# Sinkhorn-sorted attention and a token mixer on one Trainium2 core: masks ahead of a copy, wider weights for one turn, fewer idle products, a split last row and a new instruction order

## The chip, the cores and the metric

One core of a Trainium2 chip. The metric is the device time of one execution in microseconds (us). The engines are TensorE (PE, with its weight loads as PEld), VectorE (DVE), ScalarE (ACT), GpSimd (POOL) and SyncE (SP, which here only issues transfers). A core has 16 DMA engines; transfers are issued from the queues of SP, ACT and POOL. PSUM has eight banks of 512 float32 per partition. TensorE alone fills them, VectorE and ScalarE empty them.

## The reference

The input is q, k and v (4 batches, 8 heads, 768 positions, 64 wide, float32), sort_net (4, 8, 8, 8) and three matrices. The first half sorts blocks of 96 positions with a soft permutation P and attends inside each block; the second mixes tokens with weights made from the attention's output:

```python
P = sort_net
for _ in range(5):
    P = np.exp(P - np.max(P, axis=-1, keepdims=True))
    P = P / (np.sum(P, axis=-1, keepdims=True) + 1e-09)
    P = P / (np.sum(P, axis=-2, keepdims=True) + 1e-09)
k_sorted = np.einsum('bhij,bhjcd->bhicd', P, k_b)      # v_sorted likewise
attn = softmax(scale * q_b @ k_sorted^T)               # per block of 96
x = attn @ v_sorted                                    # (4, 768, 512)
W_tok = scale * (x @ w_q) @ (x @ w_k)^T
out = np.maximum(W_tok @ x, 0) @ w_out
```

## The kernel before, in words

The whole program is one list, ORDER (lines 20 to 54), read word by word by the loop at lines 661 to 671. A capital letter is a group of products on TensorE, and its number behind the colon is the PSUM bank; the small letter of the same name empties that bank, on ScalarE (A), VectorE (D) or POOL (G); a word that begins with l is a load issued by POOL. The first digit is the batch, the rest says which part. So K20:6 is the sorted k of batch 2, head pair 0, into banks 6 and 7, and k20:A its copy by ScalarE. Each engine takes its words in the order of the list, and waits there until what a word needs is ready; a word that waits holds up all later words of its engine. Bank numbers and engines are written out by hand for each word.

The groups that the change or the prediction's steps touch:

- **a and c** (lines 171 and 183): the softmax chain that makes P. a is an exponential on ScalarE, c the sums, reciprocals and products on VectorE; they alternate five times. A (line 179) makes a small mask m_p; Z (line 257) multiplies zeros (idle products; the last digits of the name count them, so Z04 is four).
- **I, z, Q, q** (lines 266, 342, 262 and 274): q of batch 0 comes by I, two transfers from SP's queue; z1n casts it; Q turns one head pair by an identity product, and q copies it to QT. For batches 1 to 3 the copy p (line 271) puts the two heads of a pair side by side first; it waits for POOL's load lq.
- **B, u, n** (lines 235, 242, 245): B00 spreads P over 128 partitions in one bank. u00 copies that bank to PTR in SBUF on ScalarE. n makes the masks M that sort k and v: those of batch 0 (n00 to n03, two heads each) read the bank itself, on VectorE; those of batches 1 to 3 read PTR, on POOL.
- **K/k, Y/y, F/f, V/v, R** (lines 289 to 331): sorted k; sorted v of batch 0, which is turned once more by F; sorted v of the other batches (V), moved to VT by six transfers R on SP's queue.
- **S/e, P/r/x** (lines 352 to 395): scores in seven groups and their exponentials; the products with v in five groups, the reciprocal of the sums and the product that makes X.
- **T/t or D, J/j, d, W/w, G/g, H/h** (lines 397 to 462): X is turned on TensorE (T) or by a transposing transfer (D); J makes q' and k' (qkT, 64 rows each); d moves k' to the other half of the partitions (qD); W turns k' back in eight blocks of 96 columns, by a product with an identity; G and H make the mixed and rectified tokens, mixT.
- **O/o/s** (lines 464 to 488): the last product in six rows per batch, its copy out of PSUM and its store. For batch 3 each row has its own store. A number from 10 up means half of a row's columns (osplit), so 325 is the second half of row 5 and 315 the first half.

POOL's loads go into three buffers each of q, k and v (NIN, line 112), each half of a batch (four heads) by itself: lk0a is the first half of k of batch 0. At the end POOL checks the reciprocals (guard, line 495); with this input the slow path behind it isn't taken.

Of the kernel before, what the change touches and what calls it, by code (L numbers as in the profile page):

```python
# [17 lines left out]
VHEAD = set()  # L18

ORDER = """  # L20
i00:G i02:D I00:S A00:0 lv0b I01:S Z04:1 lk0a c00:D a01:A i03:G c01:D lv0a a02:A:0 lk0b c02:D z11:A
lv1b lv1a a03:A Q01:0 c03:D lk1a z10:A a04:A c04:D Z22:1 z12:A Q00:2 q01:D:0 a05:A z13:A Z32:3 c05:D
q00:A:2 Q03:0 Z52:1 q03:D:0 B00:2 Q02:3 u00:A:2 n01:D:2 Z12:0 n00:D:2 n11:G K01:4 n03:D:2 K00:0
q02:D:3 k01:A:4 Y03:6 n10:G k00:D:0 y03:A:6 S02:4 n02:D:2 e02:A:4 Y00:0 lq1b K02:2 Y02:6 y00:A:0
k02:D:2 Y01:4 lk1b y02:A:6 S00:0 y01:D:4 lp K03:2 e00:A:0 S01:6 k03:D:2 F00:4 lq1a e01:A:6 F01:5
f00:D:4 S06:2 S05:0 e06:A:2 f01:D:5 P00:6 e05:A:0 S03:2 r00:D:6 x00:D:6 V12:4 e03:A:2 P01:0 r01:D:0
x01:D:0 v12:A:4 S04:6 F03:2 F02:3 e04:A:6 R15:S V11:4 f02:D:3 V10:0 v11:A:4 f03:D:2 P02:6 p12:G
Z42:3 v10:A:0 r02:D:6 x02:D:6 R12:S p13:G Z62:4 P04:2 R14:S K11:4 n20:G T00:0 r04:D:2 x04:D:2
k11:A:4 R13:S Q12:1 P03:6 R11:S t00:A:0 q12:D:1 lk2a K13:2 r03:D:6 x03:D:6 R10:S Q13:1 k13:A:2 lv2b
K12:4 U00:0 k12:A:4 lv2a K10:2 z01:D:0 T03:6 q13:D:1 k10:A:2 T02:7 t03:D:6 U01:4 p11:G T01:5 t02:D:7  # L30
z02:A:4 S16:2 S14:0 t01:D:5 lo e16:A:2 S15:6 Q11:4 e15:A:6 p10:G J01:5 q11:D:4 J00:2 e14:A:0 n21:G
S13:6 j00:D:2 j01:A:5 Q10:0 e13:A:6 W01:1 lq2a W00:1 P14:2 P13:4 w00:A:1 d01:G r14:D:2 x14:D:2
q10:A:0 K20:6 lq2b G00:1 r13:D:4 x13:D:4 k20:A:6 lq3a S11:2 G01:1 e11:A:2 d00:G K21:6 g00:D:1 S10:4
lk2b k21:D:6 H01:0 e10:A:4 h01:D:0 V20:2 V21:4 v20:A:2 V22:6 v21:D:4 P10:0 v22:A:6 R21:S T13:2
r10:D:0 x10:D:0 R20:S H02:4 S12:6 O02:3 R25:S e12:A:6 h02:D:4 R23:S H00:0 o02:A:3 P12:6 R22:S
h00:A:0 O03:3 p21:G r12:D:6 x12:D:6 R24:S t13:A:2 P11:4 lk3a O04:0 r11:D:4 x11:D:4 p20:G O00:2
o04:A:0 lv3a p23:A T10:0 o00:D:2 lv3b Q21:1 p22:A Q20:4 q21:D:1 T11:2 n31:G q20:A:4 T12:5 t11:D:2
O05:1 t12:A:5 o03:D:3 lq3b t10:D:0 S22:6 S20:4 e22:A:6 S21:2 lk3b o05:D:1 J11:0 p30:G e21:A:2 Q23:1
j11:D:0 J10:6 p31:G q23:D:1 e20:A:4 Q22:7 j10:D:6 W11:1 n30:G Q30:0 q22:A:7 K22:4 q30:D:0 K23:2
k22:A:4 Q31:0 s01:G k23:D:2 W10:1 P21:6 d10:G w10:A:1 d11:D S23:4 q31:D:0 S24:2 e23:A:4 O01:1  # L40
r21:D:6 x21:D:6 e24:A:2 S25:4 G10:0 o01:D:1 e25:A:4 K31:6 K30:2 k31:D:6 G11:0 k30:A:2 P22:4 g10:D:0
S26:2 r22:D:4 x22:D:4 V30:0 e26:A:2 P23:6 v30:A:0 H10:2 r23:D:6 x23:D:6 V31:4 h10:A:2 R30:S p33:G
S31:0 R31:S v31:D:4 e31:A:0 p32:G V32:6 H12:2 v32:A:6 S32:0 h12:D:2 R33:S Q33:4 Q32:5 e32:A:0 R32:S
K32:6 q33:D:4 R34:S P24:2 k32:A:6 K33:0 r24:D:2 x24:D:2 R35:S k33:A:0 P20:6 q32:D:5 D21:S H11:2
S35:0 r20:D:6 x20:D:6 h11:A:2 O14:5 e35:A:0 S33:2 o14:D:5 D20:S S36:6 O13:4 e33:A:2 P31:0 s00:S
e36:A:6 S34:2 r31:D:0 x31:D:0 P34:6 e34:A:2 O10:5 r34:D:6 x34:D:6 P32:2 o10:A:5 S30:0 r32:D:2
x32:D:2 P33:6 e30:A:0 J20:5 J21:0 r33:D:6 x33:D:6 j20:A:5 P30:2 d20:G j21:A:0 W20:5 r30:D:2 x30:D:2
d21:G W21:5 D31:S O12:6 w20:A:5 G21:5 o13:D:4 D30:S G20:5 o12:D:6 O11:4 g20:D:5 s11:S H20:6 s02:S
H22:2 h20:A:6 H21:0 h22:D:2 O15:5 o11:A:4 O21:6 o15:D:5 h21:A:0 s10:G O20:7 J30:0 J31:1 j30:D:0
O25:5 d30:G j31:D:1 d31:S W30:4 o20:D:7 W31:4 O22:1 w30:A:4 w31:A:4 o25:D:5 o21:A:6 G31:0 s12:A  # L50
G30:0 s20:A O23:6 o22:A:1 g30:A:0 H30:0 o23:D:6 H31:4 h30:A:0 H32:2 h31:D:4 O24:7 s21:S h32:A:2
O31:6 o24:A:7 O32:2 o31:D:6 s22:S O34:3 s31:A o32:D:2 O35:6 s32:A o34:A:3 O30:7 o35:D:6 s34:S O33:3
s35:A o30:D:7 s30:S o33:A:3 s33:S
"""


# [1 line left out]
def kernel(  # L58
# [23 lines left out]
    DH = moe_w_q.shape[1]  # L82
# [40 lines left out]
    qkT = tiles("qkT", 2, [P, S])  # L123
# [6 lines left out]
    q32 = [x.rearrange("p t s -> p (t s)").bitcast(FP32).rearrange("p (h r d) -> p h r d", r=R6, d=D) for x in XT]  # L130
# [10 lines left out]
    idb = sb.tile([P, P], BF16, name="idb")  # L141
# [11 lines left out]
    def mm(o, w, x, start=True, stop=True, t=False):  # L153
        nc.tensor.matmul(o, w, x, is_transpose=t, start=start, stop=stop, skip_group_check=True)  # L154
# [267 lines left out]

    def u_W(b, n, bank):
        for i in range(4 * n, 4 * n + 4):
            mm(PS[0:BLK, bank, i * DH:(i + 1) * DH], qkT[b % 2][:, i * BLK:(i + 1) * BLK], idb[:, DH:P])

    def u_w(b, n, e, bank):
        i0, i1 = (4 * n, 4 * n + 4) if b == B - 1 else (0, NB)
# [232 lines left out]
    for item in ORDER.split():  # L661
# [5 lines left out]
        b, n = int(name[1]), int(name[2:])  # L667
# [41 lines left out]
```

## Time and profile before

| | us |
|---|---|
| median of 3 timed runs | 99.87 |
| lowest and highest | 98.56, 100.75 |
| the profiled execution's own time | 98.28 |
| its span in the profile | 96.3 |
| busy in it: PE, PEld, DVE, ACT, POOL | 83.7, 57.7, 72.4, 68.8, 43.1 |

The profile lists the instructions of one execution, grouped by line, engine and shape, or in order of time. A row of the timeline has start, duration, engine, line, operation, what it writes and reads, and in brackets how long its engine had stood idle before it and what ended that. Line 154 is the helper through which all products go, lines 158, 160 and 162 those of the copies, so these rows are told apart by the names of their tiles. "fil" is the tile of zeros that the idle products use. Neighbouring rows of one group are merged, with a count behind the x.

### The profile page before, as it was taken

What the parts mean: (1) busy time and instruction counts of PE and PEld (TensorE: products, weight loads), DVE (VectorE), ACT (ScalarE), POOL (GpSimd) and SP (SyncE); (2) the same over time, 40 slices, a digit from 0 to 9 for tenths busy, and PEclk for the clock granted to TensorE, in tenths of its full rate; (3) what the DMA queues carried; (4) which work ended last, traced back from release to release, by engine and by line L of the source; (5) the groups of instructions that cost most, each with busy time, mean ns of one, the idle gap of its engine ahead of it and who ended that gap; (6) DMA issues with size and microseconds to landing.
All of it is one profiled execution on the core that took longest, in us unless ns stands there. A gap on an engine that the chain in (4) does not pass through costs nothing.

```text
span 96.3 us, 3183 instructions
## 1 busy us (share of the span) xinstructions
PE 83.7 (87%) x1322; PEld 57.7 (60%) x1332; DVE 72.4 (75%) x141; ACT 68.8 (72%) x96; POOL 43.1 (45%) x70
## 2 busy tenths in 40 slices
PE   4429488999999999899999999899989999999930
PEld 2024177888788687855868687675666645644400
DVE  2667987988799469999777999998698773645520
ACT  5267739998789899886989898999766090466220
POOL 6993069800999994049999004200004021950000
PEclk9999999999999999999999999999999999999999
DMA  1899999999999999999999999659961998385992
GB/s 10 262 356 228 203 202 203 203 202 208 194 276 229 208 205 206 202 202 232 251 231 204 202 205 274 188 140 218 180 244 32 225 353 361 119 354 221 395 367 113
DMA packets 24656, 21.44 MB, mean 223 GB/s; under 512 B 7297, under 2 KB 22721, under 8 KB 24641
## 3 DMA queue, kind: packets, MB, share of 16 engines
q0 software_dynamic: 12720, 10.36, 65.6%
q1 hardware_dynamic: 11200, 9.05, 32.5%
q10 hardware_dynamic: 720, 1.84, 4.8%
q8 instruction: 10, 0.16, 0.7%
q14 instruction: 6, 0.04, 0.1%
HBM read 20.19 MB, written 6.29 MB: 275 GB/s over the span
## 4 chain that ended last, share of the span: by engine, by line
PE 58%; DVE 14%; ACT 14%; DMA 5%; issue 4%; SPq 0%; DVEq 0%; ACTq 0%
PE ps L154 58%; ACT E L363 5%; DMA XT<-in_q_dram 5%; DVE X L392 5%; ACT KT L158 3%; ACT Vs L158 3%; DVE QT L162 2%; DVE Vs L162 1%; DVE Rall L387 1%; DVE XT L162 1%; ACT mixT L460 1%; ACT Qn L158 1%; DVE tmp L193 1%; DVE Pm L190 1%; DVE tmp L189 1%
## 5 line engine op out<-in xcount | busy, mean ns | idle before, releaser
L363 ACT ACTIVATE E<-ps 96x960 bf16<-96x960 f32 (+1 forms) x28 | 24.3, 905 | 2.3 <-PE ps L154 1.6
L154 PE MATMUL ps<-wo,mixT 128*128 128x512 bf16 x88 | 22.8, 380 | 0.4
L392 DVE TENSOR_TENSOR X<-ps,Rall 96x896 bf16<-96x896 f32 (+1 forms) x20 | 20.1, 1007 | 0.7
L160 POOL COPY Qn<-Qn 128x768 bf16<-128x768 bf16 x10 | 8.1, 829 | 17.1 <-DMA Qn<-in_q_dram 17.0
L162 DVE COPY ot<-ps 128x512 f32<-128x512 f32 (+1 forms) x16 | 10.8, 687 | 4.8 <-PE ps L154 4.1
L154 PEld LDWEIGHTS <-mixT 128*128 128x128 bf16 x96 | 8.3, 98 | 9.1 <-issue 0.8
L154 PE MATMUL ps<-idb,Qn 128*128 128x128 bf16 x96 | 8.4, 231 | 4.4 <-ACT Qn L158 3.1
L158 ACT CAST KT<-ps 128x768 bf16<-128x768 f32 x13 | 10.1, 806 | 2.3 <-PE ps L154 1.8
L154 PE MATMUL ps<-VT,E 96*128 96x65 bf16 x256 | 11.1, 193 | 0.2
L154 PEld LDWEIGHTS <-E 96*128 96x128 bf16 x256 | 9.8, 97 | 2.1 <-ACT E L363 0.4
L154 PEld LDWEIGHTS <-KT 64*128 64x128 bf16 (+1 forms) x288 | 8.4, 97 | 4.1 <-issue 2.2
L154 PEld LDWEIGHTS <-Qn 128*128 128x128 bf16 x96 | 6.2, 103 | 7.5 <-ACT Qn L158 6.8
L253 POOL TENSOR_TENSOR M<-PTR,m_p 128x512 bf16<-128x512 bf16 x6 | 7.9, 1316 | 5.0 <-ACT PTR L158 4.9
L154 PE MATMUL ps<-QT,KT 64*128 64x96 bf16 x256 | 9.3, 204 | 0.7 <-ACT KT L158 0.2
L460 ACT ACTIVATE mixT<-ps 128x1024 bf16<-128x1024 f32 x7 | 7.1, 1027 | 3.5 <-PE ps L154 3.5
L160 POOL COPY qD<-qkT 64x384 bf16<-64x384 bf16 x6 | 3.0, 504 | 14.5 <-ACT qkT L158 12.2
L158 ACT COPY ot<-ps 128x512 f32<-128x512 f32 x9 | 5.3, 587 | 5.1 <-PE ps L154 4.7
L154 PE MATMUL ps<-M,Kn 128*64 128x128 bf16 x192 | 7.8, 221 | 0.3 <-DVE M L253 0.3
L158 ACT CAST Vs<-ps 128x1024 bf16<-128x1024 f32 x7 | 7.0, 1016 | 0.5 <-PE ps L154 0.3
L162 DVE CAST KT<-ps 128x768 bf16<-128x768 f32 x7 | 6.5, 952 | 1.0 <-PE ps L154 0.9
L387 DVE RECIPROCAL Rall<-ps 96x14 f32<-96x14 f32 (+1 forms) x20 | 4.6, 229 | 3.5 <-PE ps L154 1.8
L162 DVE COPY QT<-ps 128x768 bf16<-128x768 bf16 x12 | 6.6, 546 | 0.7 <-PE ps L154 0.7
(84 smaller groups left out, 140.8 us busy)
## 6 DMA issues: line engine op xcount, KB each, us to landing
Vn<-in_v_dram POOLq DMA_DIRECT2D x8, 384.0 KB, 9.6
Kn<-in_k_dram POOLq DMA_DIRECT2D x8, 384.0 KB, 10.3
out_dram<-ot SPq DMA_DIRECT2D x5, 512.0 KB, 4.6
VT<-Vs SPq DMA_DIRECT2D x18, 132.0 KB, 5.3
Qn<-in_q_dram POOLq DMA_DIRECT2D x6, 384.0 KB, 10.8
XT<-in_q_dram SPq DMA_DIRECT2D x2, 768.0 KB, 5.8
out_dram<-ot POOLq DMA_DIRECT2D x2, 512.0 KB, 7.5
out_dram<-ot ACTq DMA_DIRECT2D x2, 512.0 KB, 2.8
```

The lines of the kernel that those rows point to most:

```text
L154: nc.tensor.matmul(o, w, x, is_transpose=t, start=start, stop=stop, skip_group_check=True)
L158: nc.scalar.copy(o, i)
L160: nc.gpsimd.tensor_copy(o, i)
L162: nc.vector.tensor_copy(o, i)
L189: nc.vector.reciprocal(tmp, tmp)
L190: nc.vector.tensor_mul(Pv, Pv, rows(tmp))
L193: nc.vector.reduce_sum(tmp, (Pm if n == 1 else Pv).rearrange("p i j -> p j i"), axis=AX.X)
L253: ENG[e].tensor_tensor(out=M[b % 2][:, h0:h0 + hn], in0=src.unsqueeze(2).to_broadcast([P, hn, SP, NB]), in1=m_p.unsqueeze(1).unsqueeze(3). ...
L363: nc.scalar.activation(E[b % 2][:, n, 0:2 * w * BLK].rearrange("p (t a c) -> p a t c", a=2, c=BLK), PS[0:BLK, bank:bank + 2, 0:w * BLK].re ...
L387: nc.vector.reciprocal(Rall[:, b, n, :, 0:w], avps(bank, w)[:, :, :, D])
L392: nc.vector.tensor_mul(xo.rearrange("p (a t d) -> p a t d", a=2, d=D), avps(bank, w)[:, :, :, 0:D], Rall[:, b, n, :, 0:w].unsqueeze(3).to_ ...
L460: nc.scalar.activation(o, i, ACT.Relu)
```

## The change

- ORDER is written anew: all positions, most banks, and for 67 words the engine. Seven groups of idle products (16 products) become four (10): Z42, Z52 and Z62 are gone, the other four are placed differently. The masks n00 to n03 of batch 0 come ahead of u00. POOL's first memsets (i03) come ahead of all loads, and the loads have another order; batch 0's q comes in the order I01, I00.
- Row 5 of batch 3 (O35, o35, s35) is cut into two halves of columns (325 and 315), which come last of all; both half copies are on VectorE and both half stores on ScalarE's queue.
- u_W reads 128 columns of k' as weights instead of 96, except for each fourth block; the products write 128 rows instead of 96, of which the copy w reads 96 as before.

```diff
--- before.py
+++ after.py
@@ -18,39 +18,39 @@
 VHEAD = set()
 
 ORDER = """
-i00:G i02:D I00:S A00:0 lv0b I01:S Z04:1 lk0a c00:D a01:A i03:G c01:D lv0a a02:A:0 lk0b c02:D z11:A
-lv1b lv1a a03:A Q01:0 c03:D lk1a z10:A a04:A c04:D Z22:1 z12:A Q00:2 q01:D:0 a05:A z13:A Z32:3 c05:D
-q00:A:2 Q03:0 Z52:1 q03:D:0 B00:2 Q02:3 u00:A:2 n01:D:2 Z12:0 n00:D:2 n11:G K01:4 n03:D:2 K00:0
-q02:D:3 k01:A:4 Y03:6 n10:G k00:D:0 y03:A:6 S02:4 n02:D:2 e02:A:4 Y00:0 lq1b K02:2 Y02:6 y00:A:0
-k02:D:2 Y01:4 lk1b y02:A:6 S00:0 y01:D:4 lp K03:2 e00:A:0 S01:6 k03:D:2 F00:4 lq1a e01:A:6 F01:5
-f00:D:4 S06:2 S05:0 e06:A:2 f01:D:5 P00:6 e05:A:0 S03:2 r00:D:6 x00:D:6 V12:4 e03:A:2 P01:0 r01:D:0
-x01:D:0 v12:A:4 S04:6 F03:2 F02:3 e04:A:6 R15:S V11:4 f02:D:3 V10:0 v11:A:4 f03:D:2 P02:6 p12:G
-Z42:3 v10:A:0 r02:D:6 x02:D:6 R12:S p13:G Z62:4 P04:2 R14:S K11:4 n20:G T00:0 r04:D:2 x04:D:2
-k11:A:4 R13:S Q12:1 P03:6 R11:S t00:A:0 q12:D:1 lk2a K13:2 r03:D:6 x03:D:6 R10:S Q13:1 k13:A:2 lv2b
-K12:4 U00:0 k12:A:4 lv2a K10:2 z01:D:0 T03:6 q13:D:1 k10:A:2 T02:7 t03:D:6 U01:4 p11:G T01:5 t02:D:7
-z02:A:4 S16:2 S14:0 t01:D:5 lo e16:A:2 S15:6 Q11:4 e15:A:6 p10:G J01:5 q11:D:4 J00:2 e14:A:0 n21:G
-S13:6 j00:D:2 j01:A:5 Q10:0 e13:A:6 W01:1 lq2a W00:1 P14:2 P13:4 w00:A:1 d01:G r14:D:2 x14:D:2
-q10:A:0 K20:6 lq2b G00:1 r13:D:4 x13:D:4 k20:A:6 lq3a S11:2 G01:1 e11:A:2 d00:G K21:6 g00:D:1 S10:4
-lk2b k21:D:6 H01:0 e10:A:4 h01:D:0 V20:2 V21:4 v20:A:2 V22:6 v21:D:4 P10:0 v22:A:6 R21:S T13:2
-r10:D:0 x10:D:0 R20:S H02:4 S12:6 O02:3 R25:S e12:A:6 h02:D:4 R23:S H00:0 o02:A:3 P12:6 R22:S
-h00:A:0 O03:3 p21:G r12:D:6 x12:D:6 R24:S t13:A:2 P11:4 lk3a O04:0 r11:D:4 x11:D:4 p20:G O00:2
-o04:A:0 lv3a p23:A T10:0 o00:D:2 lv3b Q21:1 p22:A Q20:4 q21:D:1 T11:2 n31:G q20:A:4 T12:5 t11:D:2
-O05:1 t12:A:5 o03:D:3 lq3b t10:D:0 S22:6 S20:4 e22:A:6 S21:2 lk3b o05:D:1 J11:0 p30:G e21:A:2 Q23:1
-j11:D:0 J10:6 p31:G q23:D:1 e20:A:4 Q22:7 j10:D:6 W11:1 n30:G Q30:0 q22:A:7 K22:4 q30:D:0 K23:2
-k22:A:4 Q31:0 s01:G k23:D:2 W10:1 P21:6 d10:G w10:A:1 d11:D S23:4 q31:D:0 S24:2 e23:A:4 O01:1
-r21:D:6 x21:D:6 e24:A:2 S25:4 G10:0 o01:D:1 e25:A:4 K31:6 K30:2 k31:D:6 G11:0 k30:A:2 P22:4 g10:D:0
-S26:2 r22:D:4 x22:D:4 V30:0 e26:A:2 P23:6 v30:A:0 H10:2 r23:D:6 x23:D:6 V31:4 h10:A:2 R30:S p33:G
-S31:0 R31:S v31:D:4 e31:A:0 p32:G V32:6 H12:2 v32:A:6 S32:0 h12:D:2 R33:S Q33:4 Q32:5 e32:A:0 R32:S
-K32:6 q33:D:4 R34:S P24:2 k32:A:6 K33:0 r24:D:2 x24:D:2 R35:S k33:A:0 P20:6 q32:D:5 D21:S H11:2
-S35:0 r20:D:6 x20:D:6 h11:A:2 O14:5 e35:A:0 S33:2 o14:D:5 D20:S S36:6 O13:4 e33:A:2 P31:0 s00:S
-e36:A:6 S34:2 r31:D:0 x31:D:0 P34:6 e34:A:2 O10:5 r34:D:6 x34:D:6 P32:2 o10:A:5 S30:0 r32:D:2
-x32:D:2 P33:6 e30:A:0 J20:5 J21:0 r33:D:6 x33:D:6 j20:A:5 P30:2 d20:G j21:A:0 W20:5 r30:D:2 x30:D:2
-d21:G W21:5 D31:S O12:6 w20:A:5 G21:5 o13:D:4 D30:S G20:5 o12:D:6 O11:4 g20:D:5 s11:S H20:6 s02:S
-H22:2 h20:A:6 H21:0 h22:D:2 O15:5 o11:A:4 O21:6 o15:D:5 h21:A:0 s10:G O20:7 J30:0 J31:1 j30:D:0
-O25:5 d30:G j31:D:1 d31:S W30:4 o20:D:7 W31:4 O22:1 w30:A:4 w31:A:4 o25:D:5 o21:A:6 G31:0 s12:A
-G30:0 s20:A O23:6 o22:A:1 g30:A:0 H30:0 o23:D:6 H31:4 h30:A:0 H32:2 h31:D:4 O24:7 s21:S h32:A:2
-O31:6 o24:A:7 O32:2 o31:D:6 s22:S O34:3 s31:A o32:D:2 O35:6 s32:A o34:A:3 O30:7 o35:D:6 s34:S O33:3
-s35:A o30:D:7 s30:S o33:A:3 s33:S
+i00:G i02:D I01:S i03:G A00:0 I00:S Z04:1 c00:D lk0b a01:A c01:D lk0a lv0a a02:A:0 lv0b c02:D lv1b
+z13:A lv1a a03:A Q03:0 c03:D lq1b z12:A lk1b a04:A q03:A:0 Z12:1 c04:D z10:A Q02:0 a05:A z11:A Z22:1
+c05:D q02:A:0 Q00:2 q00:D:2 B00:0 Q01:1 n03:D:0 n01:D:0 q01:A:1 K03:2 n00:D:0 K01:4 k03:A:2 n02:D:0
+K00:6 k01:D:4 u00:A:0 K02:2 k00:A:6 n10:G S05:0 k02:D:2 Y01:4 e05:A:0 Y00:6 y01:D:4 S01:2 lq1a Z32:0
+e01:A:2 y00:D:6 lp S04:4 Y03:0 e04:A:4 Y02:2 n11:G S00:6 y02:D:2 y03:A:0 F00:4 F01:5 e00:A:6 f00:D:4
+lk1a S02:2 f01:D:5 V11:0 e02:A:2 n20:G S03:6 v11:D:0 S06:4 e06:A:4 P01:2 e03:A:6 F02:4 r01:D:2
+x01:D:2 R13:S p12:G V12:0 V10:6 v12:A:0 p13:G f02:D:4 P00:2 v10:A:6 Q12:5 R15:S r00:D:2 x00:D:2
+F03:4 R14:S Q13:0 q12:A:5 K13:6 R10:S f03:D:4 P02:2 k13:A:6 R12:S T00:1 q13:D:0 p11:G r02:D:2
+x02:D:2 t00:A:1 R11:S S15:6 P03:4 e15:A:6 lv2a K12:0 r03:D:4 x03:D:4 U00:2 p10:G k12:A:0 P04:6 T01:3
+lv2b S16:0 z01:D:2 S14:4 e16:A:0 r04:D:6 x04:D:6 T02:2 n21:G e14:A:4 Q11:0 U01:1 t02:D:2 Q10:6
+q11:A:0 t01:D:3 T03:7 lk2a K11:4 t03:D:7 z02:A:1 K10:2 k11:D:4 J01:7 k10:A:2 n30:G J00:1 q10:D:6
+j01:A:7 lo S10:6 j00:A:1 S11:2 e10:A:6 W01:4 W00:4 lq2a P13:0 w00:D:4 e11:A:2 S12:6 d01:G r13:D:0
+x13:D:0 G01:4 lq3a e12:A:6 G00:4 lk2b S13:2 d00:D g00:D:4 P14:0 e13:A:2 V22:6 r14:D:0 x14:D:0 V20:4
+v22:A:6 H01:2 v20:D:4 K20:0 h01:A:2 V21:6 k20:D:0 R20:S K21:4 v21:A:6 H00:2 R25:S k21:D:4 P12:0
+h00:A:2 R21:S P11:6 r12:D:0 x12:D:0 H02:4 R24:S O03:2 h02:A:4 R22:S r11:D:6 x11:D:6 P10:0 R23:S
+O02:3 p21:A p20:G r10:D:0 x10:D:0 T11:6 o02:A:3 n31:G T13:7 Q21:4 o03:A:2 Q20:5 t13:D:7 T12:2
+q21:D:4 lq2b q20:A:5 O05:7 t11:D:6 p30:A p31:G t12:D:2 S21:4 S22:0 o05:D:7 e21:A:4 S20:2 lk3b T10:6
+O04:7 lv3b e20:A:2 t10:D:6 J11:6 lv3a o04:A:7 J10:2 j11:A:6 e22:A:0 Q30:3 j10:D:2 K22:6 K23:4
+q30:A:3 k22:D:6 P21:0 k23:A:4 O00:2 r21:D:0 x21:D:0 p23:A p22:G W11:3 Q31:4 W10:3 o00:A:2 Q23:5 lk3a
+q31:D:4 P20:0 w10:A:3 q23:D:5 Q22:4 lq3b r20:D:0 x20:D:0 S26:2 S25:6 e26:A:2 s01:G G10:5 e25:A:6
+K32:2 d11:G q22:D:4 G11:5 d10:G k32:D:2 K33:0 g10:A:5 P24:6 k33:A:0 H11:4 r24:D:6 x24:D:6 H10:2
+h11:A:4 H12:0 h10:D:2 S24:6 h12:A:0 V32:4 v32:D:4 V31:2 e24:A:6 S23:0 e23:A:0 v31:D:2 V30:6 R35:S
+K31:4 R34:S v30:A:6 K30:0 k31:D:4 P22:2 R33:S k30:A:0 O11:6 r22:D:2 x22:D:2 R30:S p32:G p33:A R32:S
+P23:0 o11:A:6 S31:4 R31:S r23:D:0 x23:D:0 S30:2 e31:A:4 Q33:6 D20:S O10:7 e30:A:2 q33:D:6 Q32:0
+o10:D:7 D21:S S32:4 S36:2 q32:D:0 O01:6 e36:A:2 e32:A:4 s10:S S33:2 S34:0 e33:A:2 P30:4 O14:7
+r30:D:4 x30:D:4 e34:A:0 P31:2 o01:A:6 S35:0 r31:D:2 x31:D:2 P32:4 s00:G e35:A:0 J20:6 o14:A:7
+r32:D:4 x32:D:4 P34:0 J21:2 j20:A:6 d20:G P33:6 j21:A:2 r34:D:0 x34:D:0 D30:S W20:4 W21:4 O13:5
+w20:A:4 r33:D:6 x33:D:6 d21:A G21:4 G20:4 o13:D:5 D31:S O12:6 g20:A:4 H20:4 s02:S H21:0 h20:A:4
+H22:2 O15:7 h22:D:2 h21:A:0 O21:4 o12:D:6 o15:A:7 O23:5 s11:S s12:G J30:7 J31:6 j30:A:7 o21:A:4
+O20:0 j31:A:6 W30:4 d31:S W31:4 O22:1 w30:D:4 w31:D:4 d30:S o20:D:0 G30:4 o23:D:5 G31:4 s20:S O24:0
+o22:D:1 g30:A:4 s21:G H31:4 H32:6 h31:A:4 H30:2 O25:1 h30:D:2 o24:A:0 O33:4 o25:D:1 O30:5 o33:D:4
+s22:A h32:A:6 O32:1 s33:S o30:D:5 O31:0 s30:A o32:A:1 O34:5 o31:D:0 s32:S O325:4 s31:S o34:A:5
+O315:0 o325:D:4 s34:A o315:D:0 s325:A s315:A
 """
 
 
@@ -422,7 +422,8 @@
 
     def u_W(b, n, bank):
         for i in range(4 * n, 4 * n + 4):
-            mm(PS[0:BLK, bank, i * DH:(i + 1) * DH], qkT[b % 2][:, i * BLK:(i + 1) * BLK], idb[:, DH:P])
+            w = BLK if i % 4 == 3 else P
+            mm(PS[0:w, bank, i * DH:(i + 1) * DH], qkT[b % 2][:, i * BLK:i * BLK + w], idb[:, DH:P])
 
     def u_w(b, n, e, bank):
         i0, i1 = (4 * n, 4 * n + 4) if b == B - 1 else (0, NB)
```

## The prediction

> **What bounds the kernel now.** I read the page first (busy times, clock, the chain's shares), then busy times by stage, then the timeline at each edit. From the page:
>
> ```profile
> span 96.3 us, 3183 instructions
> PE 83.7 (87%) x1322; PEld 57.7 (60%) x1332; DVE 72.4 (75%) x141; ACT 68.8 (72%) x96; POOL 43.1 (45%) x70
> PEclk9999999999999999999999999999999999999999
> DMA  1899999999999999999999999659961998385992
> PE 58%; DVE 14%; ACT 14%; DMA 5%; issue 4%; SPq 0%; DVEq 0%; ACTq 0%
> ```
>
> TensorE is the largest share of the chain that ends last, VectorE and ScalarE are not far behind, the clock is never down, and the transfer engines are busy without a gap from slice 2 to slice 27 (about 2.4 to 65 us). Busy time by stage comes next, from the first sorted k (13.3) to the end of the last product (about 92.0); columns are start:end, length, then busy time of PE, PEld, DVE, ACT, POOL, clock, transfer share, GB/s.
>
> ```profile
> 13.30:30.60 17.30, 16.32 (x387) 14.45 (x389) 15.47 (x27) 15.42 (x20) 11.80 (x15) 1.00 1.28 215
> 59.40:73.20 13.80, 12.86 (x230) 9.23 (x231) 11.96 (x20) 11.87 (x16) 1.58 (x3) 1.00 0.80 188
> 73.20:92.00 18.80, 18.64 (x142) 9.61 (x142) 11.48 (x17) 8.26 (x14) 5.07 (x11) 1.00 0.77 275
> sum 78.70, PE 76.04 PEld 54.27 DVE 63.38 ACT 61.06 POOL 35.48; mean PE 15.21 PEld 10.85 DVE 12.68 ACT 12.21 POOL 7.10
> ```
>
> Over 78.7 us TensorE stands still for 78.70 - 76.04 = 2.7 us, almost all of it in the first row (17.30 - 16.32 = 1.0) and the second (13.80 - 12.86 = 0.9). In the first row the two engines that empty PSUM are busy for 15.47 and 15.42 of 17.30, so that stage is held by all three; in the last row TensorE alone sets the end. So a new order can win back at most 2.7 us, and there is little in it unless the two stages with gaps change.
>
> **First masks.** The timeline around the first masks:
>
> ```profile
> 11.99 0.51 DVE L162 COPY QT<-ps 128x768 bf16<-128x768 bf16 x1
> 12.12 0.36 PE L154 MATMUL ps<-PbT,Lx 32*128 32x32 bf16 x8 [0.15 <-DVE PbT L197]
> 12.51 0.37 ACT L158 CAST PTR<-ps 128x256 bf16<-128x256 f32 x1 [0.85 <-PE ps L154]
> 12.91 1.09 DVE L253 TENSOR_TENSOR M<-ps,m_p 128x256 bf16<-128x256 f32 x3 [0.42 <-ACT PTR L158]
> 13.28 0.82 PEld L154 LDWEIGHTS <-Kn 128*64 128x64 bf16 x24 [0.42 <-issue]
> ```
>
> The mask on VectorE stands idle for 0.42 us until ScalarE's copy of the same bank ends at 12.88, though it reads only the bank. In the new order the masks come first, so the copy's 0.4 us leave the path. But a q copy (0.51, the row at 11.99) now stands on VectorE between the end of the softmax chain and the masks: chain end about 12.1, plus 0.55, gives 12.65 instead of 12.91. I take -0.25 us; the bounds are -0.4 (the whole wait) and 0 (a q copy now stands on ScalarE between the fourth and the fifth exponential and could delay the chain by as much). The copy in turn now comes behind four masks, 4 x 0.36 us, and POOL's masks of batch 1 and the scores that want bank 0 come behind the copy; this takes nothing off the first sorted k, which needs only its own mask. [...]
>
> **No idle products late.** Seven groups of products into unused columns become four: six products fewer.
>
> ```profile
> 23.35 1.28 DVE L162 COPY VT<-ps 96x1024 bf16<-96x1024 bf16 x2 [0.26 <-PE ps L154]
> 24.38 0.56 PEld L154 LDWEIGHTS <-fil 128*128 128x128 bf16 x4
> 25.06 0.50 PEld L154 LDWEIGHTS <-E 96*128 96x128 bf16 x8
> ```
>
> Two of the six stand ahead of B00, in TensorE's wait for the softmax: worth 0. The other four run from 24.38 to 25.06: 0.68 us at most. The products that follow (E, eight of them) want the bank that VectorE's copy leaves at 23.35 + 1.28 = 24.63, so they could have begun 0.4 us earlier. Against that, one of the groups that stay (Z32) moves from the softmax, where it cost nothing, to a place behind the second group of scores of batch 0: two products, half of the 0.68, under a wait for a bank as far as I can follow, and up to 0.34 if that wait is gone. I take -0.3 for all of it; bounds +0.34 (VectorE, busy for 15.47 of 17.30, is the limit at 24.4 anyway and Z32 costs its full time) and -0.68.
>
> **k' turned by 128 columns.** Three of four weight loads of the turn of k' become 128 wide. By the rows of both widths:
>
> ```profile
> L154 PEld LDWEIGHTS <-qkT 128*96 128x96 bf16 x32 | 2.0, 124 | 0.3
> L154 PEld LDWEIGHTS <-mixT 128*128 128x128 bf16 x96 | 8.3, 98 | 9.1 <-issue 0.8 <-ACT mixT L460 0.5
> 73.18 0.58 PEld L154 LDWEIGHTS <-qkT 128*96 128x96 bf16 x8
> 26.07 0.37 PEld L154 LDWEIGHTS <-X 96*128 96x128 bf16 x8
> ```
>
> 24 loads x (124 - 98) ns = 0.62 us is the most, if the loads set the pace; eight 96-wide loads took 0.58, eight 128-wide ones with a similar stream 0.37. But weight loads run under the product before, and only two of the four batches (2 and 3) have the turn with little else beside it, so I take -0.1; bounds 0 and -0.6. [...]
>
> **Last row in halves.** The end now:
>
> ```profile
> 92.02 0.38 PE L154 MATMUL ps<-wo,mixT 128*128 128x512 bf16 x1
> 92.44 0.58 ACT L158 COPY ot<-ps 128x512 f32<-128x512 f32 x1 [1.63 <-PE ps L154]
> L446 DVE TENSOR_SCALAR Ab<-ps 128x256 bf16<-128x256 f32 x3 | 1.2, 417 | 0.1
> out_dram<-ot SPq DMA_DIRECT2D x3, 256.0 KB, 2.3
> qD<-qkT SPq DMA_DIRECT2D x1, 48.0 KB, 2.0
> ```
>
> The last product, copy and store become half as large; the copy moves to VectorE. No copy of 128x256 float32 to float32 is in the trace; the nearest, a 128x256 read of PSUM on VectorE, takes 0.42, so 0.58 - 0.42 = 0.16. The last store falls from 256 to 128 KB; 48 KB take 2.0 and 256 KB 2.3, so at most 0.3, and I take 0.2. Both half stores are issued by ScalarE, one behind the other; its queue has nothing else left. One product group, one copy and one store are added, the first half's copy under the second half's products. Sum -0.4; bounds 0 and -0.5.
>
> **The new order.** 67 items change their engine. The six more that ScalarE gets are 6 of 104, and VectorE's total hardly changes; the sum of emptying is not smaller than before, so the gaps can only be closed by better fitting. I found no such place by hand, and take 0 here, with -1.9 (both stages' gaps closed) as the lower bound. What I can follow is the loads. POOL's queue and the wait on batch 2's v:
>
> ```profile
> 27.11 0.82 POOL L232 DMA_DIRECT2D Kn<-in_k_dram  x1
> 29.49 0.82 POOL L160 COPY Qn<-Qn 128x768 bf16<-128x768 bf16 x1
> 35.06 0.36 PEld L154 LDWEIGHTS <-Kn 128*64 128x64 bf16 x12
> 37.86 0.51 PEld L154 LDWEIGHTS <-M 128*128 128x128 bf16 x9 [0.26 <-DMA Vn<-in_v_dram]
> L253 POOL TENSOR_TENSOR M<-PTR,m_p 128x512 bf16<-128x512 bf16 x6 | 7.9, 1316 | 5.0 <-ACT PTR L158 4.9
> DMA to landing us min/median/max: 6.5/10.3/15.0
> ```
>
> The last line is for the loads of k. Now the first half of k for batch 2 (lk2a) is issued at 27.11, ahead of the copy p11 that waits for q of batch 1 and runs at 29.49. In the new order it comes behind p11, lv2a, p10, lv2b and the mask n21: 0.82 + 0.82 + 0.82 + 0.82 + 1.32 = 4.6 us after that q has landed. q's place among the loads is one earlier, about 2 us (the transfer engines are full, so loads land one after another), so lk2a is issued at about 27.5 + 4.6 = 32.1 and lands no sooner than 32.1 + 6.5 = 38.6. Its user K20 stands later in TensorE's order too: it now begins at 35.06, and by the items now ahead of it that were behind it (S10, S11, S12, G00, G01, V20, V22, H01, less the idle products) would come near 37. V22 just ahead of K20 wants both halves of v, which are again two loads in the same queue, so TensorE arrives at 37 to 38 and may wait 0.6 to 1.6 there, against 0.26 now; all of TensorE's later work is queued behind. Some of this is absorbed, as the emptying engines go on meanwhile. I take +0.4; bounds 0 and +4.6 (a median landing, 32.1 + 10.3 = 42.4, against 37.5 and the 0.26 of now).
>
> **Sum.** -0.25 - 0.3 - 0.1 - 0.4 + 0.4 = -0.65 us. The profiled execution took 98.28 us, 96.3 of span and 2.0 around it, so the sum gives 97.6 against its own 98.28. The three timed runs have a median of 99.87 (98.56 to 100.75); the profiled one lies below all of them. The mean of the four is 99.4, the sum on that scale is 98.7, and this I give: **98.7 us**. About 2% (2.0 us) is what a measurement of this kernel can tell from no change.
>
> **Rivals.**
> The order fits better than I can see: the gaps at 13.3 to 30.6 and 59.4 to 73.2 close by 1.9 us and K20 doesn't wait. For it: in those rows no engine is full, so the waits are a matter of order; against it: ScalarE gets more, not less. Then -0.65 - 0.4 - 1.9 = -2.95: 96.4 us.
> The loads hand everything back: transfers are full from 2.4 to 65 us, the loads are the same in number and size, so what masks and idle products gain early is waited for again at the next load; only the halves and the turn remain, -0.5: 98.9 us. For it: the wait on v at 37.86; against it: it is the only such wait on TensorE after the start, and 0.26 us short.
> Slower: lk2a lands late and K20 holds TensorE up for longer than everything else gains. It decides from the point where the added wait exceeds the other gains (1.05 us), that is when lk2a lands after 37.5 + 0.26 + 1.05 = 38.8. Its price is halfway between the 0.6 and the 4.6 above, +2.6, less 1.05: +1.55, 100.9 us. For it: five POOL items moved ahead of this load, and a median of 10.3 us to landing; against it: that median was for loads issued behind a longer queue.
> That the edit does nothing: the 96-wide loads and the removed products were under other work already, and the masks' gain is eaten by the softmax chain, which has one more q copy on ScalarE inside it; the time is 99.4 less the halves' 0.4, 99.0, and its chance is counted with the second rival's.
>
> **How the numbers follow.** Forecast 0.38, better order 0.24, loads hand it back 0.20, late K20 0.18. The range reaches the better order (96.4) and the late K20 (100.9): 96.3 to 101.0, which leaves out the far halves of both, 0.12 + 0.09; the forecast's own range is 97.7 to 99.7. Faster by over 2%, a gain of 2.0 us: nearly all of the better order and a fifth of the forecast, since the base itself scatters by 1 us either way: 0.24 x 0.9 + 0.38 x 0.2 = 0.29, say 0.3. Slower by over 2% takes a wait of 3.1 us at K20, which is under half of that rival, and a little of the scatter: 0.13. The rest, 0.57, lies within.
>
> **What would show it.** Masks: the first M on VectorE begins near 12.65 with no wait on PTR, and PTR begins after the last of four. Idle products: none after 20 us. Turn: a row of qkT loads of 128 columns near 98 ns. End: a copy of 128x256 near 0.42 us last, and span end under 3.9 us after the last product. Loads: a wait of TensorE on Kn's load between 36 and 40 us of 0.6 to 1.6. The prediction is wrong if TensorE's idle time from the first sorted k to the last product is below 1.5 us or above 4.5, or if the first sorted k starts after 13.3.

## The result, and the profile after

The changed kernel takes 101.9 us (median of 4, 101.34 to 102.1) against 99.23 for the one before (98.56 to 100.75): a ratio of 1.032, 95% interval 1.026 to 1.037. It is slower; 98.7 was forecast, in a range of 96.3 to 101.0. Ratios compare, for each kernel, the executions that lie near its fastest, so a ratio can differ from the quotient of two medians; why the kernel before spreads from 98.2 to 102 is taken up in runs 7 and 9. The profiled execution of the changed kernel took 101.87, with a span of 99.9. From its page:

```profile
span 99.9 us, 3193 instructions
PE 84.8 (85%) x1321; PEld 59.9 (60%) x1330; DVE 72.0 (72%) x139; ACT 71.2 (71%) x102; POOL 41.7 (42%) x68
PEclk9999999999999999999999999999999999999985
DMA 38%; PE 24%; DVE 17%; POOL 5%; ACT 5%; issue 4%; SPq 1%; DVEq 0%; POOLq 0%; ACTq 0%
```

Less work, and yet TensorE is busy for 84.8 us instead of 83.7: something runs more slowly. The granted clock doesn't show it (1.00 in the first row below), and falls only when the products are over (0.79 in the last). The chain's share for transfers follows POOL's queue of loads and says little of the cause. Busy time by stage, the same stretches as before and the rest:

```profile
13.30:30.60 17.30, 16.80 (x357) 14.54 (x357) 14.82 (x23) 15.01 (x19) 12.86 (x15) 1.00 1.27 205
59.40:73.20 13.80, 12.05 (x223) 8.81 (x225) 11.89 (x17) 12.31 (x16) 1.37 (x2) 1.00 0.97 254
92.00:99.90 7.90, 2.14 (x14) 1.18 (x12) 1.54 (x3) 1.05 (x2) 0.00 (x0) 0.79 0.54 203
```

In the first stretch TensorE is busy for longer (16.80 after 16.32) with fewer products (357 after 387). The second has 1.75 us of standstill after 0.94; the difference is the wait for the transposed X of batch 2 at J20, first before, then changed:

```profile
PEld L154 <- DMA XT<-X: 0.5, 1, 0.5
PE ps L154 <- DMA XT<-X: 1.3, 1, 1.3
```

The third is the end: it lasts 7.9 us, in the kernel before 4.3 (96.3 - 92.0). By the last copy out of PSUM the changed kernel is 1.6 us behind (94.61 for 93.02); the other 2.0 us come after that copy.

**The start.** TensorE's timeline up to the first sorted k, first of the kernel before, then of the changed one:

```profile
6.62 0.82 PE L154 MATMUL ps<-idb,Qn 128*128 128x128 bf16 x6 [3.14 <-ACT Qn L158]
7.23 1.06 PE L154 MATMUL ps<-fil 128*128 128x512 bf16 x2
8.08 0.85 PE L154 MATMUL ps<-idb,Qn 128*128 128x128 bf16 x6
8.72 1.06 PE L154 MATMUL ps<-fil 128*128 128x512 bf16 x2
11.02 0.51 PE L154 MATMUL ps<-idb,Qn 128*128 128x128 bf16 x6 [1.24 <-DVE Pm L190]
...
13.39 0.81 PE L154 MATMUL ps<-M,Kn 128*64 128x128 bf16 x22 [0.26 <-DVE M L253]
```

```profile
6.90 0.82 PE L154 MATMUL ps<-idb,Qn 128*128 128x128 bf16 x6 [3.42 <-ACT Qn L158]
7.51 1.06 PE L154 MATMUL ps<-fil 128*128 128x512 bf16 x2
9.49 0.80 PE L154 MATMUL ps<-idb,Qn 128*128 128x128 bf16 x6 [0.92 <-ACT QT L158]
...
12.64 0.82 PE L154 MATMUL ps<-idb,Qn 128*128 128x128 bf16 x6
13.39 2.77 PE L154 MATMUL ps<-M,Kn 128*64 128x128 bf16 x48
```

The same six q products take 0.82 us until 9 us and 0.51 at 11.02 in the kernel before; in the changed one they still take 0.82 at 12.64. There 48 products of the sorted k take 2.77 us, where 22 took 0.81: pairs start every 106 ns instead of every 55. The products of the first sorted v go at the same pace until 17.8; from 18.03 on it is the full one. So TensorE works at half its rate in the changed kernel until 18 us. In the kernel before the four groups from 6.62 to 9.8 follow each other without a gap; in the changed one Q02 waits 0.92 us, from 8.57 on, for the copy of Q03, since the new order gives both bank 0.

The idle products, 512 columns wide, show two rates as well: in the kernel before their starts lie 427 ns apart at 8.72 and 216 at 11.37. The time to the rise is not one number here: 5.5 us after the last gap (12.31) in this execution, and 2.9 us in run 11. That the gaps hold the rise back is at this point the author's reading; runs 1, 4 and 9 test it.

**The end.** The first row of POOL's check in the kernel before, and then POOL's, VectorE's and ScalarE's rows of the last microseconds in the changed one:

```profile
82.14 0.76 POOL L500 CROSS_LANE_REDUCE s<-Rall 96x1 f32<-96x280 f32 x1
```

```profile
87.22 0.53 POOL L486 DMA_DIRECT2D out_dram<-ot  x1 [5.61 <-DVE ot L162]
87.81 0.76 POOL L501 CROSS_LANE_REDUCE s<-Rall 96x1 f32<-96x280 f32 x1
...
93.75 0.86 DVE L162 COPY ot<-ps 128x256 f32<-128x256 f32 x2 [0.61 <-PE ps L154]
...
93.92 1.37 ACTq L489 DMA_DIRECT2D out_dram<-ot  x3
```

POOL's check of the reciprocals started at 82.14 before. Now the stores s12 and s21 stand ahead of it on POOL; s21 waits 5.61 us for its rows and the check begins at 87.81. From the end of the last copy (93.75 + 0.86 = 94.61) to the end of the span it takes 5.3 us; before, 96.3 - 93.02 = 3.3. In the records of the trace POOL's closing instructions now end at 99.1 and the wait for the last store at 98.1; before, POOL was done at 93.4 and the wait for the last store ended at 95.3. From the check's first row to the end of POOL's closing work it is 11.3 us in both (82.14 to 93.4, 87.81 to 99.1), so that end came 5.7 us later with a check that started 5.67 us later.

### The profile page after: what moved, and what is told of

Read it like the earlier page. It is cut to its first block, busy times and chain, and to the rows that moved or that the text cites. A ratio compares the mean times of both kernels' runs of the same rounds, so it can differ in the third digit from the quotient of the medians.

```text
span 99.9 us, 3193 instructions
## 1 busy us (share of the span) xinstructions
PE 84.8 (85%) x1321; PEld 59.9 (60%) x1330; DVE 72.0 (72%) x139; ACT 71.2 (71%) x102; POOL 41.7 (42%) x68
## 3 DMA queue, kind: packets, MB, share of 16 engines
q1 hardware_dynamic: 11136, 8.57, 28.8%
## 4 chain that ended last, share of the span: by engine, by line
DMA 38%; PE 24%; DVE 17%; POOL 5%; ACT 5%; issue 4%; SPq 1%; DVEq 0%; POOLq 0%; ACTq 0%
PE ps L154 24%; DMA Qn<-in_q_dram 23%; DMA XT<-X 5%; DMA out_dram<-ot 5%; DMA XT<-in_q_dram 5%; DVE X L392 4%; POOL M L253 2%; DVE ot L162 2%; DVE VT L162 2%; POOL Qn L160 2%; DVE QT L162 1%; ACT Qn L158 1%; DVE Vs L162 1%; ACT E L363 1%; DVE Rall L387 1%
## 5 line engine op out<-in xcount | busy, mean ns | idle before, releaser
L154 PE MATMUL ps<-wo,mixT 128*128 128x512 bf16 (+1 forms) x92 | 22.5, 370 | 0.5 <-issue 0.2
L162 DVE CAST KT<-ps 128x768 bf16<-128x768 f32 x11 | 10.3, 953 | 2.5 <-PE ps L154 2.5
L461 ACT ACTIVATE mixT<-ps 128x1024 bf16<-128x1024 f32 x9 | 9.0, 1029 | 3.3 <-PE ps L154 3.3
L486 POOL DMA_DIRECT2D out_dram<-ot x4 | 2.2, 542 | 19.5 <-ACT ot L158 13.9
L162 DVE COPY ot<-ps 128x512 f32<-128x512 f32 (+2 forms) x14 | 8.9, 646 | 1.8 <-PE ps L154 1.6
L158 ACT COPY ot<-ps 128x512 f32<-128x512 f32 x12 | 6.9, 587 | 2.1 <-PE ps L154 1.9
L158 ACT CAST KT<-ps 128x768 bf16<-128x768 f32 x9 | 7.2, 800 | 0.8 <-PE ps L154 0.8
L154 PEld LDWEIGHTS <-Kn 128*64 128x64 bf16 x192 | 7.1, 125 | 1.0 <-issue 0.4
L154 PE MATMUL ps<-XT,wqk 128*128 128x384 bf16 x32 | 6.2, 326 | 1.3 <-DMA XT<-X 1.3
L158 ACT COPY QT<-ps 128x768 bf16<-128x768 bf16 x7 | 5.6, 794 | 1.8 <-PE ps L154 1.8
```

The costliest lines, as they stand in the source:

```text
L158: nc.scalar.copy(o, i)
L162: nc.vector.tensor_copy(o, i)
L461: nc.scalar.activation(o, i, ACT.Relu)
L486: ENG[e].dma_start(out=od[:, 2 * n:2 * n + 2, :], in_=oslot(b, 2 * n))
```

## The experiments

Two theories came out of this, the cold start and the late check; the rivals are given with each run. All runs were timed in five rounds beside the kernel before, runs 1 to 4, 5 to 8 and 9 to 12 on one chip each; "less than the change" is therefore a difference of two ratios, each with its own interval.

**1. The changed kernel, kept busy ahead of the first sorted k**

```diff
-... Z12:1 c04:D ... Z22:1 c05:D
+... Z14:1 c04:D ... Z24:1 c05:D
```

> The changed kernel with four idle products instead of two in each of the two groups ahead of the first sorted k (Z12 and Z22 become Z14 and Z24), so that TensorE has hardly a gap from 6.9 us on. Cold-start theory (TensorE runs at half rate until about 18 us because it is no longer kept busy before the first sorted k): pairs of K products start every 55 ns instead of 106, S01 starts at about 17.0 instead of 18.02, and the time falls by 0.7 to 1.5 us. Rival (the end is set by later waits and by the tail, so an earlier start is handed back): S01 earlier all the same, but J20 waits longer and the time falls by less than 0.4 us.

Measured: 1.012 (1.003 to 1.020), so 2.0% less than the change and more than expected. One of the seven executions took 269.31 us and one 104.41; neither is explained, and neither is in the ratio. TensorE in its profile:

```profile
12.62 0.51 PE L153 MATMUL ps<-idb,Qn 128*128 128x128 bf16 x6
13.34 1.20 PE L153 MATMUL ps<-M,Kn 128*64 128x128 bf16 x36 [0.22 <-DVE M L252]
```

36 products of k in 1.20 us, full rate, and S01 starts at 16.32 instead of 18.02. The cold start is a cause. In this profile 1.0 of the 1.7 us reaches the end of the last copy (93.63 for 94.61). Some is handed back as the rival said: TensorE's wait for the transposed X of batch 2 (J20) grows from 1.3 to 1.6 us.

```profile
PE ps L153 <- DMA XT<-X: 1.6, 1, 1.6
```

**2. The changed kernel with the check no longer behind stores**

```diff
-... s11:S s12:G ... g30:A s21:G
+... s11:S s12:S ... g30:A s21:S
```

> The changed kernel with the two stores s12 and s21 issued by SP instead of POOL, so that POOL's check of the reciprocals can start before 83 us as it did before. Theory of the late check (POOL's closing work ends last in the span): it begins about 5 us sooner and the time falls by 0.8 to 1.0 us, the end being then set by the last store. Rival (the last stores set the end in any case): less than 0.2 us.

Measured: 1.013 (1.006 to 1.020), 1.8% less than the change and twice what was expected. Its page's first line, and its last microseconds:

```profile
span 97.9 us, 3194 instructions
```

```profile
75.21 0.76 POOL L501 CROSS_LANE_REDUCE s<-Rall 96x1 f32<-96x280 f32 x1 [0.61 <-DVE Rall L387]
...
93.63 0.86 DVE L162 COPY ot<-ps 128x256 f32<-128x256 f32 x2 [0.61 <-PE ps L154]
...
93.81 1.37 ACTq L489 DMA_DIRECT2D out_dram<-ot  x3
```

The last copies and stores come at the same times as in the change (within 0.12 us); the span ends 2.0 us sooner. About 0.9 us of it is POOL's closing work, which ended 0.9 us after the last store's wait. The rest is that store itself: here its last packet is written at 96.2, in the change most are by 96.3, but some fifteen trickle in until 97.6. From the last copy to the end of the span it is 5.2 to 5.3 us in both profiles with the late check (the change, run 1) and 3.4 in all four of the new order with the early one (runs 2, 5, 6 and 12).

Why the late check slows the last store is not shown, but the transfers of the traces point to something. Two packets of 8 KB of the queue that the profile calls "instruction" follow POOL's branch behind the check. In the change (branch at 92.56) they run from 93.72 to 94.19 and from 96.84 to 97.14, among the last packets of the stores, of which none ends between 96.84 and 97.19; in run 2 (branch at 80.25) they come at 81.2 and 84.5. Run 2 also changes the queue of the two stores, and no run separates that from the check's time.

The start of this execution differs too. Its first sorted k is still cold, but the full rate is there at 16.3, and from 20 to 40 us it is 1.0 us ahead of the change; by 74 us that lead is gone. So what an earlier start is worth at the end differs from execution to execution.

**3. The kernel before with the masks first**

```diff
-... u00:A:2 n01:D:2 Z12:0 n00:D:2 n11:G K01:4 n03:D:2 K00:0
+... n01:D:2 Z12:0 n00:D:2 K01:4 n03:D:2 u00:A:2 n11:G K00:0
```

> The kernel before with only the first masks put ahead of the copy of their bank. The prediction's step: the first mask begins near 12.55 without a wait, the first sorted k 0.3 to 0.4 us earlier, the time 0.25 us less (0 to 0.4). Rival: the stage behind is held by the engines that empty PSUM, and the time doesn't move (under 0.1 us).

Measured: 1.000 (0.994 to 1.006). No gain is to be seen, but the interval doesn't exclude the 0.25 us. Run 8 shows where it goes.

**4. The kernel before without four early idle products**

```diff
-... Z22:1 z12:A ... Z32:3 c05:D
+... z12:A ... c05:D
```

> The kernel before without the idle products Z22 and Z32 (four products of 16, all before 10 us). Cold-start theory: TensorE is at half rate at 13.3 us, pairs of K products start every 106 ns, and the time grows by 0.7 to 1.8 us. Rival (these products only fill TensorE's idle time and the rate is up in any case, or the loss is made good later): less than 0.3 us.

Measured: 1.021 (1.013 to 1.028), 2.1% slower than before by this alone, a little over what was expected. TensorE in its profile:

```profile
8.05 0.82 PE L154 MATMUL ps<-idb,Qn 128*128 128x128 bf16 x6 [0.58 <-ACT Qn L158]
...
12.98 0.82 PE L154 MATMUL ps<-idb,Qn 128*128 128x128 bf16 x6
...
14.58 0.64 PE L154 MATMUL ps<-M,Kn 128*64 128x128 bf16 x8
```

The first sorted k comes at 14.58 instead of 13.39, its pairs 106 ns apart. Four products whose results nobody uses, in time that TensorE has to spare, are worth 2 us against the executions of the kernel before in which the rate is up in time.

**5. The changed kernel with both repairs**: the diffs of 1 and 2 together.

> The changed kernel with both repairs, the longer idle groups ahead of the first sorted k (Z14, Z24) and the stores s12 and s21 on SP. If the cold start and the late check are separate causes and make up the loss, the gains add: 1.032 - 0.020 - 0.018 = 0.994 of before, 98.6 us, within 0.6. Rival (both are paid out of the same 2 us at the end, or a third cause holds the end): 1.01, no better than either alone.

Measured: 1.002 (0.997 to 1.006), median 98.91. The gains of 1 and 2 add up to 3.8% and 3.0% are measured: between the two theories, nearer to the sum. What was lost is found: repaired, the changed kernel is level with the kernel before within 0.6%. Its wait at J20 stays at 1.4 us, so that loss belongs to the new order, and the parts or something else make it good.

**6. The same, and an earlier store s02**

```diff
-... r34:D:0 x34:D:0 D30:S ... H20:4 s02:S H21:0
+... r34:D:0 x34:D:0 s02:S D30:S ... H20:4 H21:0
```

> As the run before, and the store s02 ahead of D30 on SP instead of behind D31, so that its half of the output buffer is free before ScalarE's copy o21 wants it (o21 waited 0.27 us for that store, and j31 and the turn of k' stood behind it). Theory: W30's wait of 0.4 us goes, and the time falls by another 0.3 to 0.5 us. Rival: transfers at that time are full, D30 comes later by as much, and the time doesn't move.

Measured: 1.000 (0.995 to 1.005), median 98.91 again: nothing that can be told from run 5.

**7. The kernel before with its last row in halves**

```diff
-O33:3 s35:A o30:D:7 s30:S o33:A:3 s33:S
+O323:3 s35:A o30:D:7 O313:2 s30:S o323:D:3 s323:A o313:D:2 s313:A
```

> The kernel before with only its last row (row 3 of batch 3) in halves, both copies on VectorE, both stores on ScalarE's queue. The prediction's step: 0.4 us less (0 to 0.5). Rival, from the packets of the last stores in the first profiles (the write queues were full at about 400 GB/s until the last packet, and 1 KB packets moved slower than 2 KB ones): no gain, 0 to 0.2 us more.

Measured: 0.998 (0.992 to 1.004). The rival's explanation fits the packets of the changed kernel: while packets of 2 KB are written, most slices of 0.3 us up to 95.5 have 370 to 420 GB/s, and from 95.5 to 96.1, with mostly 1 KB, it is 362. The difference is small, and it was not tested alone.

This run's profile showed something else. It is the kernel before up to 90 us, and its start is another:

```profile
11.08 0.82 PE L153 MATMUL ps<-idb,Qn 128*128 128x128 bf16 x6 [1.24 <-DVE Pm L189]
...
13.02 0.82 PE L153 MATMUL ps<-idb,Qn 128*128 128x128 bf16 x6
...
14.54 0.64 PE L153 MATMUL ps<-M,Kn 128*64 128x128 bf16 x16 [0.28 <-DVE M L252]
```

Q03 at 11 us runs at half rate here (0.82 for 0.51), and the first sorted k comes at 14.54, 1.2 us later. The masks' run shows the same (first sorted k at 14.52, its execution 99.57 us), the next run the other start (13.21, 98.17 us). So whether the 3.2 us of unbroken work at 6.6 are enough differs from execution to execution, with the same words of the list up to there.

**8. The kernel before with all parts, in its own order**: the diffs of 3 and 7, without Z42 and Z62, and the 128-column turn of the change.

> The kernel before with all the parts and without the new order: masks ahead of the copy, 128-column turn, the idle products Z42 and Z62 left out (Z22, Z32 and Z52 stay), last row in halves. The prediction's steps add up to -0.25 - 0.3 - 0.1 - 0.4 = -1.05 us, 0.989. Rival (each of them lies under other work): 0.997 to 1.003. If it is slower than 1.01, one of the parts and not the order is what costs.

Measured: 1.000 (0.995 to 1.006). None of the parts does harm beyond 0.6%; what is left are the order (with the idle products' new places) and the queues. Its profile has the start of the kernel before, so the two can be compared row by row. The masks start without a wait and the first sorted k comes at 13.21 instead of 13.39, but ScalarE's copy of it starts at 13.97 (13.96 before): the bank's copy, which now has to wait for the masks, stands ahead of it on ScalarE.

```profile
13.70 0.37 ACT L156 CAST PTR<-ps 128x256 bf16<-128x256 f32 x1 [2.11 <-DVE M L251]
13.97 1.51 ACT L156 CAST KT<-ps 128x768 bf16<-128x768 f32 x2
```

The two idle groups left out bring 0.4 us from 26 us on, a lead of 0.46 us is there at 69.3, and at 72.4, behind J20, it is gone: the wait for the transposed X is 1.0 us for 0.5.

**9. The kernel before with a longer third idle group**

```diff
-... Z32:3 c05:D
+... Z35:3 c05:D
```

> The kernel before with five idle products instead of two in its third group (Z32 becomes Z35), which fill TensorE's gap from 9.6 to 11.0 us. Its own executions fall into two groups: in the profiles where Q03 runs at full rate K01 starts near 13.2, in the others near 14.5. Cold-start theory (the rate goes up only after an unbroken stretch of work, and whether 6.6 to 9.6 us is enough depends on the moment): all executions fall in the first group, none above 99.5, median 98.3. Rival (the two groups have another cause, such as when q lands): the spread from 98.2 to 101 stays.

Measured: twelve executions from 98.36 to 99.28, median 98.59. Of the kernel before, 29 executions on the same chip: 8 from 98.3 to 98.9, the other 21 from 99.7 to 101.9, median of all 99.97. The upper group is gone. Against the lower group the ratio is 0.997 (0.992 to 1.002): the products cost nothing where the rate was up anyway. Its rows:

```profile
8.67 2.34 PE L154 MATMUL ps<-fil 128*128 128x512 bf16 x5
11.00 0.81 PE L154 MATMUL ps<-idb,Qn 128*128 128x128 bf16 x6
...
12.46 0.51 PE L154 MATMUL ps<-idb,Qn 128*128 128x128 bf16 x6
...
13.45 0.86 PE L154 MATMUL ps<-M,Kn 128*64 128x128 bf16 x24 [0.26 <-DVE M L253]
```

In this execution Q03 at 11.00 is still at half rate, and the rate rises at 11.7, 5.1 us after the start of unbroken work (6.56); without the longer group it would presumably have been one of the upper ones.

**10. The same with all parts**

> The run before with all the parts of the change except the order: masks ahead of the copy, 128-column turn, Z42 and Z62 left out, last row in halves. With the spread gone, small gains can be seen: the prediction's steps say 1.05 us less than the run before, the rival (all of them under other work) 0 to 0.3 us less.

Measured: six executions from 97.75 to 98.94, median 97.99; 0.990 (0.982 to 0.998). This beats both kernels: 2 us below the median of the kernel before and 0.6 us below run 9, between the two theories. Five of the six lie below the lowest of run 9 (98.36), though the intervals of the two ratios overlap. In the two profiles T01 comes 0.39 us earlier (29.78 for 30.17), which is the two idle groups, and the end of the last copy 0.90; from there to the end of the span it is 3.4 us with the halves and 3.25 without. The longer group here, where the rate rises within it:

```profile
8.75 1.77 PE L152 MATMUL ps<-fil 128*128 128x512 bf16 x5
```

**11. The kernel before, busy from the first product on**

```diff
-... Z04:1 ... Z32:3 c05:D
+... Z010:1 ... Z35:3 c05:D
```

> The kernel before with ten idle products instead of four in the first group (Z04) and five in the third, so that TensorE works without a gap from 1.4 to 10.8 us. Theory: the rate is up by about 8 us, Q00 runs at full rate, and the time is that of the run with Z35 alone or up to 0.2 us less, as the softmax chain sets the pace until 12 us. Rival: the early products hold up the first real one by 0.2 us or more.

Measured: 0.998 (0.993 to 1.003), median 98.59, as run 9; but two of twelve executions lie at 100.1 and 100.9, for a reason that no profile shows. Nothing is gained by it. The rate does come up early:

```profile
1.61 3.60 PE L154 MATMUL ps<-fil 128*128 128x512 bf16 x10
```

At 426 ns apart the ten would take 4.47 us; in the trace the starts are 427 ns apart up to 4.12 and 216 from 4.40 on, so the rate rises about 2.9 us after TensorE's first product (1.38).

**12. The changed kernel with everything**: run 6 with Z010 at the start.

> The changed kernel with all repairs: ten idle products at the start, four in each of the next two groups, s12 and s21 on SP, s02 ahead of D30. Theory: full rate before the first sorted k in each execution, 98.2 to 98.8 us, the same as the kernel before with Z35 within 0.5. If the new order in itself is better, it is 1 us or more below that; if it is worse, above 99.3.

Measured: 0.997 (0.992 to 1.002), median 98.63, 97.98 to 100.71. It is level with the kernel before again; beside the old order with the same parts and a steady start (run 10, 97.99) it is 0.6 us slower, but the intervals overlap. Its upper executions have another cause than the start: in the profiled one, of 100.46 us, K03 comes at 12.91 and S01 at 16.14, at full rate. TensorE waits there 1.7 us for two loads of v, 0.6 for one in run 6's profile:

```profile
PE ps L153 <- DMA Vn<-in_v_dram: 1.7, 2, 1.0
```

Why these loads land later stays open.

## Why the prediction was wrong, step by step

**What fails first is a reading.** "The clock is never down" rests on the granted clock, which stands at 1.00 in stretches in which TensorE ran at half rate (13.6 to 17.0 in the changed kernel). The durations of equal products would have told: the timeline of before has six q products in 0.82 us at 6.62 and in 0.51 at 11.02, and the prediction didn't compare them. (A smaller one: the two rows with gaps hold 1.9 of the 2.7 us of standstill, not almost all.) Of its own signs of being wrong one came, narrowly: the first sorted k starts at 13.39, not before 13.3.

**No idle products late: the failing step.** "Two of the six stand ahead of B00, in TensorE's wait for the softmax: worth 0", and the four that stay were priced at most by their own time in Z32's new place. Idle products were costed only by what they take, not by what they keep up. The change leaves 0.9 us of standstill between Q03 and Q02 and 0.5 ahead of B00, and 5.5 us of work from 12.31 on run at half rate: 2.0 us by run 1, 2.1 by run 4 from the other side, each give or take 1. The gap at Q02 comes from the order, which puts two groups into one bank; that the idle products there are too few to bridge it is this step. What it said of Z42 and Z62 was right: without them what follows came 0.39 us earlier in run 10's profile, where -0.3 was taken.

**The order's term looked at the wrong queue word.** +0.4 us was for a late lk2a. POOL issued it at 30.21, not 32.1, since p11 and p10 came sooner, and TensorE began K20 at 39.78 without a wait for it:

```profile
30.21 0.80 POOL L232 DMA_DIRECT2D Kn<-in_k_dram  x1
```

```profile
39.78 0.36 PEld L154 LDWEIGHTS <-Kn 128*64 128x64 bf16 x12 [0.21 <-issue]
```

The wait that the term was for measures 0, and the slower rival, which was right in its sign, was wrong in its mechanism. What the prediction did not follow are the stores moved onto POOL ahead of the check, s12 and s21: "67 items change their engine" was summed up by busy time, and the one queue with something fixed at its end was not read to the end. Price 1.8 us by run 2; the span ends 5.7 us after the last product, where under 3.9 was foretold.

**Last row in halves**, -0.4, measures 0 within 0.6 (run 7). The copy was sized rightly (0.425 for the 0.42 taken), but a store's landing was taken from its size with empty queues, and at the end they are not (370 to 420 GB/s until 95.5 in the changed kernel): the last store lands 2.2 us after the end of the last copy with the whole row (kernel before, runs 3, 4, 9 and 11) and 2.4 with the halves (runs 7, 8 and 10), where 0.2 less was taken. In the new order with the early check it is 2.05 (runs 2, 5, 6 and 12), but there the end of the span follows 1.4 us later instead of 1.0.

**First masks**, -0.25: not seen (run 3). What failed is "this takes nothing off the first sorted k": its products start sooner, but the copy out of PSUM waits behind the bank's copy (run 8). The wait of the masks went as foretold: in the changed kernel the masks start without a wait and the copy comes behind them.

```profile
12.82 1.42 DVE L253 TENSOR_TENSOR M<-ps,m_p 128x256 bf16<-128x256 f32 x4
```

```profile
14.98 0.38 ACT L158 CAST PTR<-ps 128x256 bf16<-128x256 f32 x1
```

They start at 12.82, not 12.65, as the softmax chain ended 0.2 us later behind a later load of q in this execution; in run 2's profile, with the same words up to there, they start at 12.50.

**The turn of k'**, -0.1, was not tried alone. Its loads take what was expected:

```profile
L154 PEld LDWEIGHTS <-qkT 128*128 128x128 bf16 x24 | 1.3, 98 | 1.0 <-issue 0.2 <-ACT qkT L158 0.2
```

All parts together were put at -1.05; at a steady start they measure -0.6 (run 10 against run 9), which is hardly clear of the noise.

The last rival (the edit does nothing) is what holds for the parts at an unsteady start (run 8), and the second, that gains are handed back at the next load, was seen at J20, where it is a transposing transfer that is waited for: 0.3 us more in run 1, 0.5 in run 8.

## What to carry to other kernels

Before you take out work that "only fills a wait", compare the durations of equal products on either side of it: if they differ by about two (106 and 55 ns from pair to pair here), the filler can be what brings TensorE to its full rate, and its price is that of all work up to the next unbroken stretch that is long enough, here 2.9 to 5.5 us. Where a kernel's times fall into two groups, look in both kinds of profile for the first row that differs; here it was one group of products at 11 us, and three more fillers brought the median down by 1.4 us (99.97 to 98.59). And when an item moves to another queue, read that queue to its very end, closing work included.

## What the runs showed of the hardware that was not expected

- The granted clock of the profile doesn't show TensorE's half rate: 1.00 in 13.6 to 17.0 in the changed kernel, while pairs of products started 106 ns apart.
- 3.2 us of unbroken products (6.62 to 9.8) brought the rate up in 8 of 29 executions on one chip, if their two groups of times are taken for the two starts; work unbroken from 6.56 on left none of 12 in the upper group (run 9).
- TensorE's rate rose 2.9 us (run 11), 3.2 (run 10, 6.64 to 9.8), 5.1 (run 9) and 5.5 us (the change) after the start of unbroken work.
- A store's last packets trickled in for 1.3 us (96.3 to 97.6) where POOL's check was late, and not where it was early; two 8 KB packets of the instruction queue fell among them, and that these are the cause is not shown.
- POOL's closing work ended 11.3 us after the start of its check, at 82.14 in the kernel before as at 87.81 in the change.
